# An attention block with a gated feed-forward part: other PSUM banks, another split of the score maxima and another place for the query projections in its first query block

## The chip, the core and the metric

The kernel runs on one core of a Trainium2 chip. The metric is the device time of one execution in microseconds (us), lower being better. A profiled execution also leaves a trace of every instruction: PE is the matrix engine (PEld its weight loads), DVE the vector engine, ACT the activation engine, POOL the general engine, SP the engine that issues the DMAs.

## The reference, cut to what matters

```python
mod = (silu(c) @ w_mod).reshape(1, 6, 1, -1)          # sa, ca, ga, sb, cb, gb
h = layernorm(x) * (1 + ca) + sa                      # x: 1 x 2048 x 512
q = h @ wq   # 32 heads of 16;   k = h @ wk, v = h @ wv: one head of 16 for all
p = softmax(q @ k.T * 16 ** -0.5)
x = x + ga * ((p @ v) @ wo)
h = layernorm(x) * (1 + cb) + sb
x = x + gb * ((sigmoid(h @ w_gate) * (h @ w_up)) @ w_down)    # 512 -> 1792 -> 512
```

## The kernel before, in words

The 2048 queries are cut into 4 blocks of 512 (`b`). A block has 8 units (`u`), each of four heads, so there are 32 units; a unit has 16 steps, one for each 128 keys, so there are 512 steps (`s` in the main loop). Two kinds of score tiles are made, both 128x512 in a PSUM bank:

- `st` tiles (`st_tile`): 128 keys by 512 queries, four to a step, one for each head. ACT takes the exponential of each into `P`. The softmax maximum is already in them: rows of `qp` and `kp` hold it, so it has to be known before the unit starts.
- `sa` tiles (`a_tile`): 128 queries by 512 keys, 64 to a unit, four to a step. DVE takes the maximum of each row into `mx`. They run 76 tiles ahead (`A0`): the maxima of unit i+1 are made during unit i. After a unit's last one, `max_end` and `max_rows` bring the 16 maxima of a row together, transpose them and send them by DMA to DRAM (`mD`) and back into rows of `qp`.

`pv` multiplies `P` by the values (with a column of ones for the sum), two halves to a step, into the bank `c`. A matmul of an `st` tile uses one half of the array's rows and the `sa` tile beside it the other half, so the two run at once.

There are three stages. The **prologue** loads and normalises x, projects keys and values, makes the six modulation vectors (`pmod`, `pcol`, `prow`) and the maxima of the first unit; its order is the list `PLAN` (`q02` is the query projection of block 0, third group of eight heads; `a5` is "sa tiles up to 20"; `z3` makes modulation vector 3), but a scheduler may still move its instructions. Then comes the **main loop** of 512 steps, where instructions keep the order in which they are written. In its first 128 steps, the first query block, `light` alone decides what stands between the score tiles; after that `fill` does, with a planner that keeps a clock for each engine (`COST`, `READ`, `HALF`) and puts pairs of half-height matmuls of other work (`Couple`) where the planned clock leaves room: the attention output projection (`po`), the transposes, gate and up (`pgu`) and down (`pd`) of the block before. `pick` takes them from `main`, or from `spare`, which goes ahead of `pgu` and `pd`. What is left over is done in the **tail**, with the feed-forward part of the last block, by matmuls over the whole array (`alone`).

In the prologue's unit 0 the maxima are made by positive parts (`both`): of two key tiles a and b, PE makes a-b (keys `kd`, the differences) and b, ACT takes the positive part of a-b into `rl`, and DVE adds b and takes the maximum, since max(a, b) = b + max(a-b, 0). Everywhere else DVE takes a plain maximum of each tile.

A query projection (`q_group`) is 12 matmuls with 512 columns. Two of the 16 are made in the prologue. The other 14 are made as 7 couples in steps 2 to 120, one or two pairs of matmuls at `n % 4 == 1` of a step. Their results go to DRAM (`qD`), and from there into `qp`.

DMAs that are `paced` are taken from a list, `queue`, at most one at every second score tile; `later` appends to it. Weights (`split_weight`) are loaded through it, cut into two float16 parts by POOL, and kept or stored (`wD`). The eight PSUM banks are, in the first block: `c`, two for `st`, two and every third time a third (`c2`) for `sa`, and two for couples (`b`).

Of the kernel before, what the change touches and what calls it, by code (L numbers as in the profile page):

```python
# [9 lines left out]
F32 = mybir.dt.float32  # L10
# [17 lines left out]
NU = 8  # L28
# [7 lines left out]

PLAN = 'n1 x2 l0 k0 x3 t1 l3 e1 w0 l1 n2 w3 k1 w1 q00 n3 q01 t2 t3 e2 e3 l2 m a1 k2 a3 k3 a5 w2 a8 z3 a12 z4 a16 z2 a18 z5'

# [11 lines left out]
WSTEPS = 120  # L50
WLAST = 124

# [10 lines left out]
SWITCH = 0.84  # L63
QSKIP = 2
WAIT = 0.2
OVER = 4

PBUFS = 4
SBANKS = {"st": 2, "sa": 2}
GWB = 3  # L70
RBUFS = 4
HBUFS = 36
# [3 lines left out]
def adaln_mqa_glu_kernel(  # L76
# [25 lines left out]
    psum = {}  # L102
    coarse, third = [], [0]
    psum["ctx"] = ExitStack()
# [4 lines left out]


    def bank(name):
        return psum["b"].tile([P, 512], F32, tag="b", name=name, bufs=psum.get("n", 7))

    def sbank(name):
        if name == "sa" and coarse:
            third[0] = (third[0] + 1) % 3
            if third[0] == 0:
                return cbank2("c2")
        return psum["s"].tile([P, 512], F32, tag=name, name=name, bufs=SBANKS[name]) if "s" in psum else bank(name)

# [3 lines left out]
    def cbank2(name):  # L124
        return psum["b"].tile([P, 512], F32, tag="c2", name=name, bufs=1)

# [173 lines left out]

    def split_weight(src, hi, lo, shape):
# [15 lines left out]
        later("w", lambda: load(0), lambda: load(1), split)  # L317

# [109 lines left out]
    def passes(ah, al, bh, bl):  # L428
        return ((ah, bh), (ah, bl), (al, bh))
# [102 lines left out]
    def a_tile(i, n):  # L532
        qp, pr0 = get_q(i)
        if i not in mxs:
            mxs[i] = wp.tile([P, 4, 4, 4], F32, tag="mx", name="mx", bufs=2)
            if i == 0:
# [165 lines left out]


    def weight_jobs():
        jobs = []
# [18 lines left out]
        for k in [*range(4, NFC), *range(4)]:  # L724
            jobs.append(lambda k=k: split_weight(w_down[k * P:(k + 1) * P, :], lambda: wdh[:, k], lambda: wdl[:, k], [D]))
        return jobs
# [15 lines left out]
    def ffn_groups(b):  # L742
# [116 lines left out]
        def down_group(t, lo):  # L859
            def term(n, rs):  # L860
                f, i = lo + n // 3, n % 3
                g_, w_ = passes(*gT[f], wdh, wdl)[i]
                return g_[rs, t * P:(t + 1) * P], w_[rs, f, :]
# [92 lines left out]
    psum["s"] = psum["ctx"].enter_context(tc.tile_pool(name="pa", bufs=1, space=PSUM, reuse_waits="tile"))  # L956
    psum["b"], psum["n"] = psum["s"], 6 - sum(SBANKS.values())
    pinned.append(True)
# [38 lines left out]

    banks = {"st": [0.0, 0.0], "sa": [0.0, 0.0, 0.0]}
    vq = []
# [45 lines left out]


    def light(n):
        if n % 4 == 1:
            c_, k = divmod(n // 4 - QSKIP, 17)
            if n // 4 >= QSKIP and c_ < len(early):  # L1050
                ats = [0, *(12 * (z + 1) // 9 for z in range(9)), *(12 + 12 * (z + 1) // 8 for z in range(8))]
                clock["pe"] += ats[k + 1] - ats[k]
                ready(READ - 1)
                early[c_].part(ats[k], ats[k + 1])
        elif n % 2 == 0 and vq and NKB * vq[0][0] + vq[0][1] <= n // 4 - LAG - (n % 4 == 0):
            clock["pe"] += SWITCH
            do_pv()

    def fill(n):
        if n < 4 * NU * NKB:  # L1060
            return light(n)
        if coarse:
            coarse.clear()
            banks["sa"].pop(0)
        while True:
# [15 lines left out]
    for i, (b, u) in enumerate(units):  # L1081
# [4 lines left out]
        for kb in range(NKB):  # L1086
# [45 lines left out]
    psum["b"] = psum["ctx"].enter_context(tc.tile_pool(name="pz", bufs=1, space=PSUM, reuse_waits="tile"))  # L1132
    psum["n"] = 7
    del psum["s"]
# [42 lines left out]
```

## Time and profile before

| | |
|---|---|
| time, median of 3 runs | 1740.71 us (1738.91 to 1744.54) |
| profiled execution, its own time | 1734.11 us |
| its span, first to last instruction | 1732.3 us |
| mean granted clock of TensorE | 0.984 |
| PE busy | 1650.6 us (95%) |
| DVE busy | 1462.8 us (84%) |
| ACT busy | 1293.4 us (75%) |
| POOL busy | 589.9 us (34%) |

A busy share is an average over the stages, so it tells little by itself. The views that matter are those of one stage: the busy times of a stretch, and the instructions of an engine in order of time, where the distance from one start to the next tells what a step costs.

### The profile page before, as it was taken

The numbers are of one execution on the slowest core, as the hardware profiler recorded it, in microseconds if no ns is written. First come the engines' busy times: TensorE is split into PE (matmuls) and PEld (weight loads), VectorE is DVE, ScalarE is ACT, GpSimd is POOL, SyncE is SP. The second block draws the span as 40 slices with busy tenths as digits, with TensorE's granted clock in tenths as the row PEclk, the third lists the DMA queues.
The fourth block names the chain that finished last, engine by engine and source line by source line (L and its number), as shares of the span: only waits on it lengthen the run. The fifth ranks groups of instructions, "written<-read, shape, count | busy, mean of one in ns | idle before, by whom it ended". The sixth has DMA issues, their size and how long they took to land.

```text
span 1732.3 us, 91155 instructions
## 1 busy us (share of the span) xinstructions
PE 1650.6 (95%) x41276; PEld 966.7 (56%) x41276; DVE 1462.8 (84%) x2490; ACT 1293.4 (75%) x2265; POOL 589.9 (34%) x654
## 2 busy tenths in 40 slices
PE   5889999999899999999999999999999999999998
PEld 3323333232455776767766767777657776654443
DVE  8589999999999999999899999999999999953211
ACT  3668888788878888888778888888888888885100
POOL 4303444444364321331353322332263222230433
PEclk9779999999999999999999999999999999999999
DMA  7002222322302110110202110110212110121211
GB/s 262 28 25 62 84 87 83 89 90 67 83 21 61 48 33 20 44 49 8 72 22 61 51 33 27 39 39 17 63 34 57 45 32 24 45 58 40 75 59 49
DMA packets 112284, 94.76 MB, mean 55 GB/s; under 512 B 27296, under 2 KB 102560, under 8 KB 111896
## 3 DMA queue, kind: packets, MB, share of 16 engines
q1 hardware_dynamic: 111896, 88.94, 17.2%
q8 instruction: 323, 5.29, 1.3%
q14 instruction: 65, 0.53, 0.1%
HBM read 67.95 MB, written 16.48 MB: 49 GB/s over the span
## 4 chain that ended last, share of the span: by engine, by line
PE 79%; DVE 9%; ACT 5%; issue 4%; DMA 2%; POOL 1%; SPq 1%; POOLq 0%; ACTq 0%; DVEq 0%
PE c L137 24%; PE st L137 15%; PE pgu L137 12%; PE sa L137 10%; DVE mx L137 5%; PE pd L137 5%; PE pgu L195 4%; ACT P L137 3%; PE pd L195 3%; PE pq L137 2%; PE po L137 1%; PE sa L175 1%; PE pmod L278 1%; DVE mm L137 0%; POOL ot L875 0%
## 5 line engine op out<-in xcount | busy, mean ns | idle before, releaser
L137 ACT ACTIVATE P<-st 128x512 f32<-128x512 f32 x2048 | 1181.5, 597 | 246.1 <-PE st L137 100.4
L137 DVE TENSOR_REDUCE mx<-sa 128x1 f32<-128x512 f32 x1802 | 1172.8, 687 | 71.5 <-PE sa L137 39.0
L137 PE MATMUL st<-qp,kp 64*32 64x512 f16 (+1 forms) x6656 | 864.7, 379 | 19.6 <-ACT P L137 8.5
L137 PE MATMUL sa<-kp,qp 64*32 64x512 f16 (+1 forms) x6182 | 768.8, 380 | 14.5 <-DVE mx L137 8.5
L137 PE MATMUL c<-P,V 64*32 64x256 f32 (+1 forms) x14336 | 706.2, 380 | 3.9 <-issue 2.9
L137 PEld LDWEIGHTS <-kp 64*32 64x32 f16 (+1 forms) x6656 | 275.7, 92 | 258.8 <-issue 172.4
L137 PEld LDWEIGHTS c<-P,V 64*32 64x32 f32 (+1 forms) x14336 | 324.9, 106 | 136.3 <-issue 92.7
L137 PEld LDWEIGHTS <-qp 64*32 64x32 f16 (+1 forms) x6352 | 302.3, 90 | 120.5 <-issue 52.9
L137 PE MATMUL pgu<-h2h,gw 64*32 64x512 f16 x5248 | 290.5, 377 | 2.0 <-issue 1.1
L137 PEld LDWEIGHTS <-gw 64*32 64x32 f16 x7872 | 163.3, 92 | 51.2 <-issue 19.0
L137 PE MATMUL pgu<-h2l,gw 64*32 64x512 f16 x2624 | 170.2, 377 | 0.8 <-issue 0.5
L846 POOL TENSOR_SCALAR th<-th 128x512 f32<-128x512 f32 x41 | 25.3, 617 | 368.9 <-ACT th L137 357.9
L137 DVE TENSOR_REDUCE mx<-c 128x1 f32<-128x512 f32 x170 | 116.0, 683 | 4.2 <-PE c L137 3.8
L313 POOL TENSOR_SCALAR wst<-wst 128x512 f32<-128x512 f32 x46 | 28.4, 618 | 200.4 <-DMA wst<-in_B_w_gate_dram 78.0
L508 POOL MEMSET qp<- 32x2048 f16 x32 | 57.6, 1799 | 86.2 <-PE st L137 66.0
L137 PE MATMUL pd<-wdl,gh 64*32 64x512 f16 x1120 | 78.3, 377 | 0.7 <-issue 0.7
L137 PE MATMUL pd<-wdh,gh 64*32 64x512 f16 x1120 | 78.4, 377 | 0.0
L137 PE MATMUL pd<-wdh,gl 64*32 64x512 f16 x1120 | 76.1, 376 | 0.0
L869 POOL TENSOR_TENSOR ot<-ot,gb 128x512 f32<-128x512 f32 x10 | 12.8, 1281 | 173.6 <-ACT ot L137 173.5
L195 PE MATMUL pgu<-h2h,gw 128*128 128x512 f16 x240 | 71.8, 379 | 0.0
L840 ACT ACTIVATE th<-pgu 128x512 f32<-128x512 f32 x15 | 9.0, 597 | 80.8 <-PE pgu L195 80.8
L137 PE MATMUL c<-kp,qp 64*128 64x512 f16 x170 | 66.2, 389 | 1.1 <-DVE mx L137 1.1
(173 smaller groups left out, 1467.2 us busy)
## 6 DMA issues: line engine op xcount, KB each, us to landing
gw<-wD SPq DMA_DIRECT2D x224, 128.0 KB
wD<-gw SPq DMA_DIRECT2D x56, 128.0 KB
wm<-in_w_mod_dram SPq DMA_DIRECT2D x6, 1024.0 KB
qp<-qD SPq DMA_DIRECT2D x96, 64.0 KB
xall<-in_A_x_dram SPq DMA_DIRECT2D x4, 1024.0 KB
qD<-q SPq DMA_DIRECT2D x32, 128.0 KB
raw<-cs SPq DMA_DIRECT2D x128, 32.0 KB
xr<-in_A_x_dram SPq DMA_DIRECT2D x32, 128.0 KB
```

The source lines that it names most:

```text
L137: return keep(f_(out_, *a, **k))
L175: pe.matmul(out_[cut], l_[:, cut], r_, start=start, stop=stop)
L195: pe.matmul(self.bank, l_, r_, start=(n == 0), stop=(n == self.n - 1))
L278: pe.matmul(p_[32 * k:32 * (k + 1)], cbc[:, k, :], wmods[i][:, k, :], start=True, stop=True)
L313: pool.tensor_scalar(w_, w_, SW, 0.0, op0=ALU.mult, op1=ALU.add)
L508: pool.memset(qp[j:j + 32], 0.0)
L840: act.activation(th, p_, AF.Tanh, scale=0.5 / (SH * SW))
L846: pool.tensor_scalar(th, th, 1.0, 1.0, op0=ALU.add, op1=ALU.mult)
L869: pool.tensor_tensor(ot, ot, mods2['gb'], op=ALU.mult)
```

## The change

In the first block the banks are shared out again: `st` turns through three of them and `sa` through four, and none is left for couples. After that block the numbers are as before (two for `st`, two for `sa`, one `c2`, two for couples).

Units 1 to 8, whose maxima are made in the prologue's end and in the first block, use positive parts for a quarter of the pairs of tiles (`h == qt`).

Six more query projections are in the prologue's list. The other eight are four couples in `spare`, taken by the planner behind the first block; the branch in `light` that placed the seven couples is gone.

`later` puts weights and output stores behind all else in `queue`, and `need` takes out only what it was asked for. The last four pieces of `w_down`, which lie where the query weights are, are asked for when all 16 projections are stored, not from step 124 on.

```diff
-PLAN = '... a1 k2 a3 k3 a5 w2 a8 z3 a12 z4 a16 z2 a18 z5'
+PLAN = '... a1 k2 a3 k3 a5 w2 a7 q02 a9 z3 q03 a11 z4 q10 a13 q11 z2 a15 q12 a17 q13 a18 z5'
-SBANKS = {"st": 2, "sa": 2}
+FIRST = {"st": (0, 1, 2), "sa": (3, 4, 5, 6)}
+RINGS = {"st": (0, 1), "sa": (3, 4), "c2": (5,), "f": (6, 2)}
+LAST = ("w", "out")
...
+    def ring(name, tags):
+        at[name] = (at.get(name, -1) + 1) % len(tags)
+        t_ = tags[at[name]]
+        return psum["b"].tile([P, 512], F32, tag=f"x{t_}", name=name, bufs=1)
...
     def sbank(name):
+        if not pinned:
+            return bank(name)
+        return ring(name, FIRST[name] if coarse else RINGS[name])
...
-            queue.extend((tag, f_) for f_ in fs)
+            n = len(queue) if tag in LAST else sum(z[0] not in LAST for z in queue)
+            queue[n:n] = [(tag, f_) for f_ in fs]
     def need(tag):
-        while any(z[0] == tag for z in queue):
-            queue.pop(0)[1]()
+        for z in [z for z in queue if z[0] == tag]:
+            queue.remove(z)
+            z[1]()
...
-        both = i == 0
+        both = i == 0 or i <= NU and h == qt
...
-    early = [Couple(q_group(*z), q_group(*y)) for z, y in zip(qleft[::2], qleft[1::2])]
-    main, spare = [], []
+    main, spare = [], [Couple(q_group(*z), q_group(*y)) for z, y in zip(qleft[::2], qleft[1::2])]
...
     def light(n):
-        if n % 4 == 1:
-            c_, k = divmod(n // 4 - QSKIP, 17)
-            if n // 4 >= QSKIP and c_ < len(early):
...
-                early[c_].part(ats[k], ats[k + 1])
-        elif n % 2 == 0 and vq and ...:
+        if n % 2 == 0 and vq and ...:
             do_pv()
...
-                if wdone >= nw - 4 and s < WLAST + 3 * (wdone - nw + 4):
+                if wdone >= nw - 4 and len(qdone) < 4 * NB:
                     break
```

PE in an early step of the first block, before; `wdh` and `wdl` are the two parts of the query weights there, `h1h` the normalised input:

```order
L137 MATMUL st<-qp,kp 128x512
L137 LDWEIGHTS qp
L137 MATMUL sa<-kp,qp 128x512
L137 LDWEIGHTS wdl
L137 MATMUL pq<-h1h_215,wdl 128x512
L137 LDWEIGHTS wdl
L137 MATMUL pq<-h1h_215,wdl 128x512
L137 LDWEIGHTS wdh
L137 MATMUL pq<-h1h_221,wdh 128x512
L137 LDWEIGHTS wdh
L137 MATMUL pq<-h1h_221,wdh 128x512
L137 LDWEIGHTS kp
```

The same place of the changed program; `kd` marks a tile of differences:

```order
L141 MATMUL c<-P_1286,V 32x256 x2
L141 MATMUL c<-P_1299,V 32x256 x2
L141 LDWEIGHTS kp
L141 MATMUL st<-qp,kp 128x512
L141 LDWEIGHTS qp
L141 MATMUL sa<-kd,qp 128x512
L141 LDWEIGHTS kp
L141 MATMUL st<-qp,kp 128x512
L141 LDWEIGHTS qp
L141 MATMUL sa<-kp,qp 128x512
```

The one or two pairs of `pq` matmuls of a step are gone, the score tiles and `pv` stand as they did, and one `sa` tile in eight is made of differences.

DVE in the first block, before; `c_1154` and its like are the tiles in the third bank of the maxima:

```order
L137 TENSOR_REDUCE mx<-sa 128x1 x2
L137 TENSOR_REDUCE mx<-c_1154 128x1
L137 TENSOR_REDUCE mx<-sa 128x1 x2
L137 TENSOR_REDUCE mx<-c_1173 128x1
L137 TENSOR_REDUCE mx<-sa 128x1 x2
```

The same place of the changed program; `ISA junk,mx` adds the positive part and takes the maximum, and the row behind it reads its result out:

```order
L141 TENSOR_REDUCE mx<-sa 128x1 x9
L141 ISA junk,mx<-sa,rl 128x512
L141 ISA mx 128x1
L141 TENSOR_REDUCE mx<-sa 128x1 x5
L141 ISA junk,mx<-sa,rl 128x512
L141 ISA mx 128x1
L141 TENSOR_REDUCE mx<-sa 128x1 x5
```

Of eight tiles DVE now takes six plain maxima and one of the longer kind; the eighth is ACT's, as `rl`.

PE in the prologue behind modulation vector 4, before:

```order
L278 MATMUL pmod<-wm,cbc 32x512 x4
L288 MATMUL pcol<-sel,mod 128x1 x4
L175 LDWEIGHTS qp
L175 MATMUL sa<-kd,qp 128x512
L175 LDWEIGHTS qp
```

The same place of the changed program:

```order
L284 MATMUL pmod<-wm,cbc 32x512 x4
L294 MATMUL pcol<-sel,mod 128x1 x4
L201 LDWEIGHTS wdh
L201 MATMUL pq<-h1h_358,wdh 128x512
L201 LDWEIGHTS wdh
L201 MATMUL pq<-h1l_359,wdh 128x512
L201 LDWEIGHTS wdl
```

A whole query projection, 12 matmuls over the full array, stands ahead of the next `sa` tiles.

More of the change, by code (lines that the diff above doesn't have):

```diff
@@ L102, in adaln_mqa_glu_kernel @@
     psum = {}
-    coarse, third = [], [0]
+    coarse, at = [], {}
     psum["ctx"] = ExitStack()
@@ L106, in adaln_mqa_glu_kernel @@
     dr = ctx.enter_context(tc.tile_pool(name="dr", bufs=1, space=DRAM))
+    def ring(name, tags):
+        at[name] = (at.get(name, -1) + 1) % len(tags)
+        t_ = tags[at[name]]
+        return psum["b"].tile([P, 512], F32, tag=f"x{t_}", name=name, bufs=1)
     def bank(name):
-        return psum["b"].tile([P, 512], F32, tag="b", name=name, bufs=psum.get("n", 7))
+        return ring("f", RINGS["f"]) if pinned else psum["b"].tile([P, 512], F32, tag="b", name=name, bufs=7)
     def sbank(name):
[L115 to L119, printed above, removed]
+        if not pinned:
+            return bank(name)
+        return ring(name, FIRST[name] if coarse else RINGS[name])
     def cbank(name):
@@ L124, in cbank2 @@
     def cbank2(name):
[L125 removed]
+        return ring("c2", RINGS["c2"])
     class Ordered:
@@ L298, in mod_rows, with split_weight @@
         return g_
-    def split_weight(src, hi, lo, shape):
+    def split_weight(src, hi, lo, shape, *more_):
         w = []
@@ L315, in split @@
             pool.tensor_tensor(lo_, w_, hi_, op=ALU.subtract)
-        later("w", lambda: load(0), lambda: load(1), split)
+        later("w", lambda: load(0), lambda: load(1), split, *more_)
     def row_norm(dsts, srcs, later=False):
@@ L700, in gw_tile @@
         return P2.tile([P, 4, NDC, P], F16, tag="gw", name="gw", bufs=GWB)
+    loaded = []
     def weight_jobs():
@@ L724, in weight_jobs @@
         for k in [*range(4, NFC), *range(4)]:
-            jobs.append(lambda k=k: split_weight(w_down[k * P:(k + 1) * P, :], lambda: wdh[:, k], lambda: wdl[:, k], [D]))
+            jobs.append(lambda k=k: split_weight(w_down[k * P:(k + 1) * P, :], lambda: wdh[:, k], lambda: wdl[:, k], [D],
+                                                   lambda: loaded.append(k)))
         return jobs
@@ L861, in term @@
                 f, i = lo + n // 3, n % 3
+                assert len(loaded) == NFC
                 g_, w_ = passes(*gT[f], wdh, wdl)[i]
@@ L996, in free @@
         return max(clock[z] for z in keys) + FREE
-    banks = {"st": [0.0, 0.0], "sa": [0.0, 0.0, 0.0]}
+    banks = {z: [0.0] * len(FIRST[z]) for z in FIRST}
     vq = []
@@ L1047, in light @@
     def light(n):
-        if n % 4 == 1:
-            c_, k = divmod(n // 4 - QSKIP, 17)
-            if n // 4 >= QSKIP and c_ < len(early):
-                ats = [0, *(12 * (z + 1) // 9 for z in range(9)), *(12 + 12 * (z + 1) // 8 for z in range(8))]
-                clock["pe"] += ats[k + 1] - ats[k]
-                ready(READ - 1)
-                early[c_].part(ats[k], ats[k + 1])
-        elif n % 2 == 0 and vq and NKB * vq[0][0] + vq[0][1] <= n // 4 - LAG - (n % 4 == 0):
+        if n % 2 == 0 and vq and NKB * vq[0][0] + vq[0][1] <= n // 4 - LAG - (n % 4 == 0):
             clock["pe"] += SWITCH
@@ L1063, in fill @@
             coarse.clear()
-            banks["sa"].pop(0)
+            for z in banks:
+                banks[z] = banks[z][-2:]
         while True:
```

9 lines of the change are left out of this document (3 added, 6 removed).

## The prediction

> **What bounds the kernel now.** I read the page first, then the busy times by stage, then PE, ACT and DVE in order of time inside the stage that changes.
>
> ```profile
> PE 1650.6 (95%) x41276; PEld 966.7 (56%) x41276; DVE 1462.8 (84%) x2490; ACT 1293.4 (75%) x2265; POOL 589.9 (34%) x654
> ```
>
> Stretches follow, with the busy time of PE, PEld, DVE, ACT and POOL, the granted clock, the DMA share and GB/s: the first projections, the cold part of the prologue, the first block (from the first exp of step 0 to that of step 128), the next 32 steps, and the other 352.
>
> ```profile
> 28.50:52.40 23.90, 17.13 (x177) 11.15 (x175) 16.61 (x32) 14.09 (x23) 13.82 (x12) 1.00 0.35 116
> ...
> 72.90:100.20 27.30, 24.04 (x86) 7.50 (x85) 17.78 (x54) 13.01 (x24) 0.00 (x0) 0.50 0.01 1
> 104.20:448.40 344.20, 334.01 (x3404) 104.70 (x3407) 329.89 (x558) 288.57 (x526) 146.04 (x170) 0.98 0.25 76
> 448.40:544.60 96.20, 88.23 (x2633) 54.38 (x2633) 89.75 (x150) 78.30 (x138) 45.24 (x61) 1.00 0.19 52
> 544.60:1580.00 1035.40, 1007.48 (x34075) 705.63 (x34059) 934.62 (x1520) 860.00 (x1492) 314.49 (x330) 1.00 0.14 40
> ```
>
> In the first block PE is busy 97%, DVE 96% and ACT 84% of 344.2 us. Busy shares so close together don't say which engine sets the step, so I go down to single steps. ACT in order of time, where a row is the four exps of a step:
>
> ```profile
> 202.88 2.22 ACT L137 ACTIVATE P<-st 128x512 f32<-128x512 f32 x4 [0.24 <-PE c L137]
> ...
> 223.10 2.30 ACT L137 ACTIVATE P<-st 128x512 f32<-128x512 f32 x4 [0.29 <-PE sa L137]
> ```
>
> Eight steps lie between these rows: 20.22 / 8 = 2.53 us a step. 128 steps at that rate are 323.5; the other 20.7 of the 344.2 are waits, most of them where units meet. PE in one of these steps, which holds a single pair of query matmuls:
>
> ```profile
> 202.45 0.39 PE L137 MATMUL st<-qp,kp 64*128 64x512 f16 x1
> ...
> 204.91 0.39 PE L137 MATMUL st<-qp,kp 64*128 64x512 f16 x1
> ```
>
> That is 2.46. Seven couples have 168 pairs in 119 steps, so 1.41 a step; with 0.22 a pair (row below) the mean is 2.46 + 0.41 x 0.22 = 2.55, which is what I measured. PE sets the step while queries are in it. The last pairs stand in step 120, before 430 us, and PE and ACT behind them look so:
>
> ```profile
> 430.07 0.39 PE L137 MATMUL st<-qp,kp 64*128 64x512 f16 x1
> ...
> 430.52 0.37 PE L137 MATMUL st<-qp,kp 64*128 64x512 f16 x1
> ...
> 432.52 0.39 PE L137 MATMUL st<-qp,kp 64*128 64x512 f16 x1
> ```
> ```profile
> 429.38 2.19 ACT L137 ACTIVATE P<-st 128x512 f32<-128x512 f32 x4 [0.31 <-PE sa L137]
> ```
>
> Without queries a step is still 2.45 (430.07 to 432.52). The second `st` matmul waits to 430.52: with two banks it needs the one that the second exp of the row at 429.38 reads. That exp starts 0.49 after the first (below), at 429.87, and is through at 430.47. DVE in that place:
>
> ```profile
> 428.94 1.28 DVE L137 TENSOR_REDUCE mx<-sa 128x1 f32<-128x512 f32 x2
> 430.14 0.68 DVE L137 TENSOR_REDUCE mx<-c 128x1 f32<-128x512 f32 x1
> 430.74 1.28 DVE L137 TENSOR_REDUCE mx<-sa 128x1 f32<-128x512 f32 x2
> ```
>
> Three maxima take 1.80, so 0.60 each and 2.40 a step. The step thus has three limits side by side: PE with queries 2.46 to 2.68, two banks for exps 2.45, DVE 2.40. The change moves all three.
>
> **First block, by its parts.** *PE*: without queries a step needs 2.46 - 0.22 = 2.24. *Banks*: the third bank for `st` takes away the wait of 0.2 above. *DVE* now has six plain maxima and one positive part in two steps. The trace has positive parts only in the prologue:
>
> ```profile
> 75.98 0.69 DVE L551 CUSTOM_DVE_ANT_0 junk<-sa,rl 128x512 f16<-128x512 f32 x1 [0.17 <-DVE mx L551]
> 76.60 0.08 DVE L551 DVE_READ_ACCUMULATOR2_ANT mx<- 128x1 f32 x1
> 76.86 0.69 DVE L551 CUSTOM_DVE_ANT_0 junk<-sa,rl 128x512 f16<-128x512 f32 x1 [0.17 <-PE pmod L278]
> ...
> 96.60 0.69 DVE L551 CUSTOM_DVE_ANT_0 junk<-sa,rl 128x512 f16<-128x512 f32 x1 [0.17 <-ACT mod L280]
> 97.22 0.08 DVE L551 DVE_READ_ACCUMULATOR2_ANT mx<- 128x1 f32 x1
> 97.33 0.22 DVE L565 TENSOR_REDUCE m<-mx 128x16 f32<-128x64 f32 x1
> ```
>
> One costs 0.88 ahead of another of its kind, and 0.73 ahead of something else (96.60 to 97.33). In the new order plain maxima stand between them, so I take 0.73: 6 x 0.60 + 0.73 = 4.33 for two steps, 2.17 a step (2.24 with 0.88). *ACT* has eight exps and one positive part in two steps. Rows for its rate, a pair of exps, a lone one, six positive parts, and 38 exps near the end:
>
> ```profile
> 201.55 1.08 ACT L137 ACTIVATE P<-st 128x512 f32<-128x512 f32 x2 [0.31 <-PE sa L137]
> ```
> ```profile
> 477.42 0.60 ACT L137 ACTIVATE P<-st 128x512 f32<-128x512 f32 x1 [2.01 <-PE st L137]
> ```
> ```profile
> 79.99 3.21 ACT L549 ACTIVATE rl<-sa 128x512 f32<-128x512 f32 x6 [2.50 <-PE sa L175]
> ```
> ```profile
> 1554.38 21.84 ACT L137 ACTIVATE P<-st 128x512 f32<-128x512 f32 x38 [0.32 <-PE st L137]
> ```
>
> One exp lasts 0.60 and the second of a pair starts 1.08 - 0.60 = 0.48 to 0.49 behind the first. Positive parts come every (3.21 - 0.60) / 5 = 0.52. So ACT needs 8 x 0.49 + 0.52 = 4.44, or 2.22 a step, if nothing holds it up. The 38 exps came every 21.84 / 38 = 0.57, which is the other end: 2.59 a step. They had two banks, so I put them down to the banks.
>
> PE 2.24, ACT 2.22 and DVE 2.17 lie so close that none runs smoothly. I walked two steps by hand. PE issues score pairs at 0, 0.23, 1.12 and 1.35 and so on, and an exp starts 0.43 behind its matmul (202.45 and 202.88 above). With the positive part behind the first two exps, ACT takes up the third at 1.93 instead of 1.55, and frees that bank at 2.53, where PE wants it at 2.47, with a semaphore to wait for; about 0.2 is lost in two steps. That gives 4.47 + 0.2 = 4.67, **2.33 a step**. The waits where units meet stay at 20.7: DVE's end of a unit and the row of maxima sent through DRAM last as long as before. 128 x 2.33 + 20.7 = 318.9, **25 less** than 344.2. Bounds: 2.24 a step (37 less), 2.59 (8 more).
>
> The page "ScalarE: Activation LUTs" of the Trainium skill, in the section "What ACT_TABLE_LOAD costs", speaks against this step: it gives an ACTIVATE with immediate operands as 186 ns + 0.833 ns an element, less 93 ns of overlap, an estimate of 0.52 for 512 elements. By that ACT's nine in two steps would set the pace and most of the gain would go. This trace's pairs of exps are faster (0.49), its positive parts agree (0.52).
>
> **Prologue.** Six projections of 12 matmuls are added. Three rows: two `pmod` with a stretch of 16 maxima between them, and ten matmuls of the projections that the prologue has already, from the chain of waits.
>
> ```profile
> 74.84 1.93 PE L278 MATMUL pmod<-wm,cbc 128*32 128x512 f32 x8
> ...
> 84.38 1.94 PE L278 MATMUL pmod<-wm,cbc 128*32 128x512 f32 x8
> ```
> ```profile
> 38.89 2.16 PE pq L195 x10
> ```
>
> At the full clock a matmul is 0.216, a projection 2.6, six 15.6; at half clock twice as much, 31. The stretch of 9.54 ran at a clock of 0.50. Its own work would be about 4.8 at the full clock, and two projections would make it 10.0, or 0.5 more than now; at half clock 10.4 more. So the six cost between 2 and 31. The projections at 38.89 ran at a clock of 1.00 (first stretch above), since such matmuls are dense; I take a quarter of the way up, **8 more**. ACT has 14 and POOL 27 us free there, which hides their two copies and one subtraction each; SP has nothing else to issue there than the maxima's rows, which come behind them, so the 12 stores stay hidden.
>
> The page "TensorE: Matmul & The Clock Gate" of the Trainium skill (Part 1) says that the clock is full after about 3.4 us of busy matmuls. Here PE was busy 24.04 of 27.30 us and still had 0.50, so the trace disagrees as far as busy time goes. By that rule alone this term would be 2 and the forecast 1721.
>
> **Behind the block.** The changed order has three of the four couples at steps 127 to 142 and the last at 151 to 154; the output projection begins at step 142 instead of 137. If all 72 pairs that do not reappear elsewhere came on top, they would cost 72 x 0.216 = 15.6. But PE has room there: its feed-forward work is not ready yet, and it even waits on its way, at 469 for a DMA, so that ACT stood 2.01 idle (row at 477.42).
>
> ```profile
> 469.38 5.18 DMA rb<-lD
> ```
>
> With the couples these 32 steps carry the load of the later ones, which are 1035.4 / 352 = 2.94 each; 32 x 2.94 = 94 against 96.2 now. **2 less**, bounds 6 less (that wait gone with the later start) and 15.6 more. From step 160 on the couples of a step are the same ones, shifted by 24 pairs: nothing. These 24 are one couple of `pgu`, which is left for the tail, where PE works alone:
>
> ```profile
> 1597.64 13.61 PE pd L195 x63
> ```
>
> 24 x 13.61 / 63 = **5 more**. The reordered queue I cost at nothing: the gate and up weights are asked for by step 120 and read from 159 on, and the last of `w_down` have 40 steps. If that cover were gone, each late piece would cost a DMA's time, as at 469.38. New waits in DVE and ACT are for each other's positive parts; behind ACT's stand the exps, which the walk above has counted.
>
> **Sum.** 8 - 25 - 2 + 5 = -14. The profiled execution took 1734.1 (span 1732.3 and 1.8 around it) and would take 1720; the median of the runs is 6.6 higher, 1740.7, so I forecast **1727**.
>
> **The rivals.**
> - *ACT becomes the bound, slower.* If 0.57 is ACT's own rate, a step is 4.5 x 0.575 = 2.59, the block costs 8 more and the whole is 8 + 8 - 2 + 5 = 19 more: 1760. It decides from 2.44 a step on, where the block's gain of 11 is eaten by the other terms. For it speaks the row of 38 exps, against it the pairs at 0.49.
> - *The prologue stays cold.* 31 - 25 - 2 + 5 = 9 more: 1750. For it the clock of 0.50 now, against it the dense projections.
> - *Exps come at the rate of positive parts.* With nine ACT instructions at 0.52 two steps need 4.68, with the 0.2 lost 4.88, so 2.44 a step; the block gains 11, and 8 - 11 - 2 + 5 = 0: 1741. The same comes out if three engines within 0.07 of one another hold each other up and a step falls only to 2.46, as in the steps without queries. For it the row of six positive parts, against it again the pairs. (The ScalarE page's figure, above, leads here.)
> - *All goes smoothly.* 2.24 a step, 2 for the prologue, 4 less behind the block: 2 - 37 - 4 + 5 = -34, 1707.
>
> **How the numbers follow.** Forecast 0.54, ACT 0.13, cold prologue 0.10, the slower exps 0.13, all smooth 0.10. The forecast's own range is 1712 to 1742. The range of 8 in 10 reaches from 1705 to 1751: it takes in all but the ACT rival and a little at the ends. A measurement of this kernel tells about 0.3% (5 us) from no change. Faster: forecast and smooth, 0.64. Same: mostly the slower exps, 0.14. Slower: ACT and cold prologue, 0.22.
>
> **What would show it.** The first exp should come near 112 instead of 104.6; groups of exps and positive parts every 4.67 for two steps; the first exp of step 128 near 431; steps 128 to 160 in 94; the tail 5 longer. I am wrong if exps of the first block come no closer than 0.57 on average with ACT never idle, if the clock stays at 0.5 through the projections, or if positive parts of DVE cost 0.88 and hold PE.

## The result, and the profile after

The changed kernel took 1738.5 us (1733.06 to 1748.04, 20 runs) where the kernel before took 1741.39 (1736.12 to 1749.4, 20 runs) beside it: a ratio of 0.9987 with an interval of 0.9972 to 1.0002, so no difference that can be told. A second comparison gave 0.9988 (0.9965 to 1.0011). I had forecast 14 us less; 2 to 3 less was measured (by the ratio and by the medians). The ratios in this document go by the executions in the fast state; one execution of `e8_queue_fifo` (5510.2 us) and one of the kernel before beside the last two kernels (1753.04 us) were slow and are left out.

The profiled execution took 1735.37 us, its span was 1733.6. Its stages, in the columns of the prediction's stretches: the end of the prologue, the first block, the next 32 steps, the other 352, and from the last exp to the end.

```profile
72.90:120.40 47.50, 35.41 (x174) 12.79 (x173) 22.34 (x63) 22.04 (x39) 7.03 (x7) 0.93 0.10 34
120.40:432.40 312.00, 294.53 (x3106) 79.29 (x3112) 286.41 (x548) 295.43 (x581) 124.68 (x149) 0.99 0.25 72
432.40:535.70 103.30, 98.67 (x3172) 65.23 (x3164) 91.09 (x152) 79.86 (x141) 47.53 (x62) 1.00 0.17 50
535.70:1577.00 1041.30, 1012.55 (x34080) 700.09 (x34065) 933.97 (x1520) 858.09 (x1492) 320.48 (x339) 1.00 0.15 41
1577.00:1733.60 156.60, 150.67 (x722) 68.98 (x720) 36.81 (x68) 16.23 (x26) 50.37 (x52) 0.99 0.20 63
```

One profile of each kernel isn't enough to compare stages of this length, as the experiments soon showed. So each kernel was profiled three times; the means and their differences, in us:

| stage | before, three profiles | after, three profiles | difference | forecast |
|---|---|---|---|---|
| first exp | 104.6, 105.9, 104.2 | 120.5, 122.1, 124.3 | +17 | +8 |
| first block | 343.8, 341.1, 341.0 | 312.0, 308.4, 308.8 | -32 | -25 |
| steps 128 to 160 | 96.2, 95.5, 94.9 | 103.2, 100.1, 101.0 | +6 | -2 |
| steps 160 to 512 | 1035.6, 1039.4, 1041.7 | 1041.2, 1043.1, 1027.6 | -2, not told from 0 | 0 |
| last exp to end | 152.2, 152.2, 152.2 | 156.7, 156.7, 156.7 | +4.5 | +5 |

The differences add up to -6, and the three profiled executions are 6 us apart in the mean. The timed runs, of which there are many more, say -2 to -3. The first block gained more than forecast, and the prologue and the 32 steps behind the block took it back.

ACT in a unit of the first block of the changed kernel, in order of time (start, busy time, and no idle time in brackets anywhere):

```profile
206.04 0.59 ACT L141 ACTIVATE rl<-sa 128x512 f32<-128x512 f32 x1
206.51 3.55 ACT L141 ACTIVATE P<-st 128x512 f32<-128x512 f32 x7
209.95 0.60 ACT L141 ACTIVATE rl<-sa 128x512 f32<-128x512 f32 x1
210.42 3.69 ACT L141 ACTIVATE P<-st 128x512 f32<-128x512 f32 x7
214.01 0.59 ACT L141 ACTIVATE rl<-sa 128x512 f32<-128x512 f32 x1
```

From 206.04 to 214.01 there are 14 exps and 2 positive parts without a gap: 7.97 / 16 = 0.498 for each. Two steps hold eight exps and one positive part, so 9 x 0.498 = 4.48, or 2.24 a step. ACT is now the engine that sets the step inside a unit, at 0.50 an instruction. 128 steps of 2.24 are 287; the other 25 of the 312.0 (22 in the other two profiles) lie at the boundaries of units. The waits of PE in that block (engine, line, what it waited for, us in total, times, longest):

```profile
PE st L141 <- DMA qp<-mD: 12.3, 10, 4.5
PE c L141 <- ACT cs L141: 5.8, 7, 0.8
```

The first is the wait for the row of maxima that goes through DRAM, the second the wait for ACT's copy of a unit's sums. The longest wait for the row, 4.5, is the one ahead of the very first score tile and belongs to the prologue; inside the block there are 7.8 us in nine waits, and 4.2 and 6.5 in the other two profiles. The wait for the copy is 5.8 in all three. So neither is clearly the larger.

### The profile page after: what moved, and what is told of

The parts are those of the page before. It is cut to its first block, busy times and chain, and to the rows that moved or that the text cites. A ratio compares the mean times of both kernels' runs of the same rounds, so it can differ in the third digit from the quotient of the medians.

```text
span 1733.6 us, 91980 instructions
## 1 busy us (share of the span) xinstructions
PE 1640.1 (95%) x41612; PEld 954.3 (55%) x41612; DVE 1422.5 (82%) x2487; ACT 1308.3 (75%) x2338; POOL 585.9 (34%) x654
## 4 chain that ended last, share of the span: by engine, by line
PE 82%; DVE 6%; ACT 4%; issue 3%; DMA 2%; POOL 2%; SPq 1%; POOLq 0%; ACTq 0%; DVEq 0%
PE c L141 25%; PE f L141 20%; PE st L141 14%; PE sa L141 11%; PE pgu L201 5%; PE pd L201 3%; DVE mx L141 3%; ACT P L141 2%; DMA qp<-mD 1%; PE pq L201 1%; SPq L586 1%; DVE junk L557 1%; PE po L201 1%; PE pk L444 0%; DMA xall<-in_A_x_dram 0%
## 5 line engine op out<-in xcount | busy, mean ns | idle before, releaser
L141 DVE TENSOR_REDUCE mx<-sa 128x1 f32<-128x512 f32 x1847 | 1196.8, 686 | 96.6 <-PE sa L141 65.7
L141 PE MATMUL st<-qp,kp 64*32 64x512 f16 (+1 forms) x6656 | 848.6, 378 | 24.9 <-DMA qp<-mD 14.6
L141 PE MATMUL sa<-kp,qp 64*32 64x512 f16 (+1 forms) x6290 | 792.7, 379 | 8.1 <-DVE mx L141 5.8
L141 PE MATMUL f<-h2h,gw 64*32 64x512 f16 x5120 | 291.3, 377 | 6.9 <-issue 4.9
L141 PE MATMUL f<-h2l,gw 64*32 64x512 f16 x2560 | 170.4, 376 | 2.4 <-POOL h2l L354 1.1
L141 PE MATMUL f<-wdh,gl 64*32 64x512 f16 x1120 | 74.4, 376 | 0.3
L141 PE MATMUL f<-wdl,gh 64*32 64x512 f16 x1120 | 73.2, 376 | 0.8 <-issue 0.8
L141 PE MATMUL f<-wdh,gh 64*32 64x512 f16 x1120 | 73.4, 377 | 0.0
L861 POOL TENSOR_TENSOR gl<-th,gh 128x512 f16<-128x512 f32 x56 | 65.0, 1161 | 4.7
L860 POOL TENSOR_SCALAR gh<-th 128x512 f16<-128x512 f32 x56 | 34.9, 622 | 88.9 <-DVE th L858 45.4
```

What stands on the lines that cost most here:

```text
L141: return keep(f_(out_, *a, **k))
L860: pool.tensor_scalar(hi, th, 1.0, 0.0, op0=ALU.mult, op1=ALU.add)
L861: pool.tensor_tensor(lo, th, hi, op=ALU.subtract)
```

## The experiments

All ratios are to the kernel before, run beside it on the same chip; the changed kernel stands at 0.9987 and 0.9988. `e10_gate_first`, `e11_two_behind_gate_first` and `p_before3` ran on another chip than the other experiments.

**Which part of the first block's gain comes from what.** `e1_banks_only` makes no positive parts in the first block; `e2_two_exp_banks` keeps those and takes the third bank of `st` away.

```diff
-        both = i == 0 or i <= NU and h == qt
+        both = i == 0
```

> The changed kernel with its seven banks in the first block, but plain maxima everywhere there (positive parts in unit 0 alone). If DVE limits the step once queries and the two-bank wait are gone, a step is four maxima of 0.60, so 2.40 to 2.45 against 2.28 in the changed kernel, the first block is 16 to 20 us longer than its 312, and the whole is 15 to 20 slower than the changed kernel (ratio to before near 1.008). Rival: the banks made the whole gain and ACT is relieved of 64 positive parts; then the block stays at 312 or gets a few us shorter (ratio 0.996 to 0.999).

```diff
-FIRST = {"st": (0, 1, 2), "sa": (3, 4, 5, 6)}
+FIRST = {"st": (0, 1), "sa": (3, 4, 5, 6)}
```

> The changed kernel with two banks for exps in the first block instead of three (four for maxima, positive parts kept). If the loop matmul, exp, free bank limits a step with two banks, steps go back to 2.45, 128 x 0.17 = 22 us more in the block, ratio to before near 1.011. Rival: the two-bank wait was only a sign of DVE running late, and with a quarter of the pairs as positive parts the step stays below 2.33; then 0 to 6 more, ratio 0.999 to 1.002.

Measured: without positive parts 1.0029 (1.0009 to 1.0048), the block 318.7, which is less than the 328 to 332 expected; with two banks for exps 1.0169 (1.0147 to 1.0192), the block 339.9, which is more than expected (a ratio near 1.011). DVE of the first, in order of time, is back to back at 12.68 / 21 = 0.60 a maximum, the 2.40 a step that stood in the kernel before too. The second view is the row of its whole block, in the columns of the stretches above:

```profile
202.57 12.68 DVE L141 TENSOR_REDUCE mx<-sa 128x1 f32<-128x512 f32 x21
```
```profile
123.60:442.30 318.70, 305.64 (x3111) 72.04 (x3118) 314.48 (x547) 281.60 (x519) 125.05 (x149) 0.99 0.24 70
```

DVE is busy 314.5 of 318.7 us: its maxima run on while PE waits at the boundaries, so the boundaries are not added on top of 128 x 2.40 = 307. That is why the block was shorter than expected.

ACT of the second waits for PE in front of every group, and the ten exps between the starts at 206.25 and 212.76 take 6.51, so 2.60 a step, where 2.45 had been expected. The second view has the longest wait of PE in its block:

```profile
206.25 1.71 ACT L141 ACTIVATE P<-st 128x512 f32<-128x512 f32 x3 [0.31 <-PE sa L141]
207.85 0.59 ACT L141 ACTIVATE rl<-sa 128x512 f32<-128x512 f32 x1
208.33 1.66 ACT L141 ACTIVATE P<-st 128x512 f32<-128x512 f32 x3
210.30 2.21 ACT L141 ACTIVATE P<-st 128x512 f32<-128x512 f32 x4 [0.31 <-PE sa L141]
212.76 2.21 ACT L141 ACTIVATE P<-st 128x512 f32<-128x512 f32 x4 [0.24 <-PE sa L141]
```
```profile
PE st L141 <- ACT P L141: 11.0, 35, 0.6
```

PE waits 35 times there for an exp to free a bank; in the changed kernel's first profile that wait is 0.3 us, once.

So without the third bank for exps the block gains only 2 us of the 32 (339.9 against 342 before), although the queries are gone and DVE's maxima cheaper. Without the positive parts it loses 7 to 9 of them (318.7 against 310, and 0.0042 x 1740 = 7 in the timed runs). These shares don't add up to 32, since the limits stood side by side. What the queries cost in the block was not tested: no kernel has them there with three banks.

**What the projections cost in the prologue.** `e3_thin_prologue` issues one matmul instead of twelve for each of the six projections that were added; the rest of their sums is left out.

```diff
-            q_group(*args).alone()
+            g_ = q_group(*args)
+            g_.n = 12 if tok in ('q00', 'q01') else 1
+            g_.alone()
```

> The changed kernel, with only the first of the 12 matmuls in each of the six projections added to the prologue (66 matmuls left out, copies and stores kept). If the projections' own PE time lies on the prologue's path at nearly the full clock, the first exp comes 66 x 0.216 = 14 earlier, near 106 instead of 120.5, and the ratio to before is near 0.990. Rival: they keep the clock up, and without them PE falls back to half clock, or their copies and stores are what costs; then the first exp stays above 112 and the gain is under 8 (ratio 0.994 or more).

Measured: 0.9936 (0.9917 to 0.9955), 9 us less than the changed kernel; the first exp at 116.5. The end of its prologue:

```profile
72.90:116.50 43.60, 33.63 (x111) 9.07 (x109) 23.56 (x65) 22.75 (x42) 7.53 (x8) 0.56 0.11 37
```

The granted clock falls to 0.56 without the dense projections, from 0.93 (0.88 in the other two profiles). Taking out 66 matmuls, 14 us of PE at the full clock, brings the first exp only 4 to 8 earlier, and it stays 12 behind the kernel before. So the projections hold the clock up, as I had assumed, but neither their own time nor the clock alone makes the prologue's 17 us. The positive parts of unit 1 don't either: without them, in `e1_banks_only`, the first exp came at 123.6. What is left to test is the order in which PE's work stands.

`e6_prologue_order` has the same instructions in another order. `y3` makes the four `pmod` matmuls of vector 3 and ACT's copy, `z3` the rest, with a projection between them; `f` ends the first unit's maxima, and two projections follow it.

```diff
-... a7 q02 a9 z3 q03 a11 z4 q10 a13 q11 z2 a15 q12 a17 q13 a18 z5
+... a7 y3 q02 z3 a9 y4 q03 z4 a11 q10 a13 y2 q11 z2 a16 f q12 y5 q13 z5 a18
```

> The changed kernel with the same instructions in the prologue in another order: each projection stands between the four matmuls of a modulation vector and the column or row matmuls that wait for ACT's copy of it, and two projections stand behind the last maximum of the first unit, where the row of maxima is on its way (6.2 us from the transpose to the first score tile in the kernel before). Theory: the prologue's 16 us are the projections' own 16 us at full clock, put into PE's line where DVE's positive parts (0.87 us a pair) cannot cover them; four waits of 0.7 to 1.2 for ACT's copies and the two projections behind the last maximum would be covered, so the first exp comes 6 to 10 us earlier, at 111 to 115 instead of 120.5, and the ratio to before falls from 0.9987 to about 0.994. Rival: the projections are the work of PE that sets the prologue in any order; then the first exp stays within 3 us of 120.5.

Measured: 0.9930 (0.9906 to 0.9953), 10 us less than the changed kernel, the first exp at 112.4. The waits of PE from 70.5 us to the first score tile, in the changed kernel:

```profile
PE st L141 <- DMA qp<-mD: 4.5, 1, 4.5
PE sa L181 <- DVE mx L557: 2.5, 5, 0.8
PE pcol L294 <- ACT mod L286: 2.3, 2, 1.2
PE prow L302 <- ACT mod L286: 1.4, 2, 0.7
```

and in the other order:

```profile
PE sa L181 <- DVE mx L556: 1.6, 4, 0.8
PE st L141 <- DVE mx L558: 1.6, 1, 1.6
PE sa L181 <- ACT rl L554: 1.0, 3, 0.3
PE pmod L284 <- ACT rl L554: 0.9, 3, 0.3
```

The waits for ACT's copies (3.7) and for the row (4.5) are gone, and one of 1.6 ahead of the first score tile has come; the first exp came 8.0 earlier than in the changed kernel's first profile. So the order matters, as the theory says. A later kernel with the same prologue (`e10_gate_first`) had its first exp at 116.7, outside the 111 to 115 expected of this order; its granted clock there was 0.89, against 0.97 here. The changed kernel's two profiles at 0.88 had it at 122.1 and 124.3, so at like clocks the order is worth 5 to 8 us.

The time from one start on PE to the next, summed by kind of instruction over this part, shows the whole account in us. The last wait, from the last `sa` tile to the first score tile, stands by itself:

| | projections | `pmod`, `pcol`, `prow` | `sa` tiles | last wait | sum |
|---|---|---|---|---|---|
| before | 0 | 16.6 | 16.3 | 0.5 | 33 |
| after | 19.4 | 12.0 | 13.3 | 4.9 | 50 |
| other order | 16.4 | 8.5 | 14.6 | 1.9 | 41 |

From the transpose of the maxima to the first score tile it is 6.2 us in the kernel before and 4.7 in the changed one; but before, PE has the last modulation vector and more `sa` tiles to do in that time, and in the changed kernel nothing is left.

**Whether more lead of the maxima removes the boundary waits.** `e5_a0_80` changes one number, `A0 = 76` to 80.

> The changed kernel with the maxima one step further ahead (80 tiles instead of 76), so that the row of maxima of a unit starts one step, some 2.3 us, earlier. Theory 'the row is the wait': in the first block of the changed kernel a step costs 2.28 inside a unit, and the rest, some 12 to 15 us at the seven unit boundaries, is PE waiting for the row that is sent through DRAM (12.3 us in 10 waits in the list of waits). With a step more those waits fall to about 2, the block to about 300 from 312, and the time by 8 to 13 us, to a ratio near 0.992 of before. Rival: DVE and the copy of the sums on ACT end last at the boundary as well; then the waits for the row only change their name, and the block stays within 3 us of 312. The prologue gets four more maxima, which cost 0 to 2 us.

Measured: 0.9970 (0.9949 to 0.9990); the first block 301.8. The waits in its first block:

```profile
PE c L141 <- ACT cs L141: 3.2, 7, 0.5
PE st L141 <- DMA qp<-mD: 1.9, 5, 0.8
```

The waits for the row are 1.9 here and 4.2 to 7.8 inside the block in the changed kernel's profiles, those for the copy 3.2 and 5.8; the block fell by 7 to 10, as expected. But the end from the last exp on took 167.9 instead of 156.7: the planner left one couple more (24 matmuls) for the tail, and PE waited 2.3 there for a gate weight. The first exp at 124.0 and the 1031.1 of steps 160 to 512 lie within the spread of the changed kernel's own profiles. The time fell by 3 us, within the intervals, where 8 to 13 had been expected. `e7_order_and_a0` put both together.

> The prologue's other order and the 80 maxima ahead together. Theory: the two waits lie in different places, so the gains add: first exp near 113 to 115 (112.4, and four maxima more), first block 300 to 303, the ratio to before 0.003 to 0.006 below the 0.993 of the order alone, so 0.987 to 0.990. Rival: the step gained at the boundaries is given back by more pairs of feed-forward matmuls left for the tail (it grew by 11 with 80 maxima alone, while steps 160 to 512 fell by 10); then the ratio is 0.991 to 0.994.

Measured: 0.9956 (0.9932 to 0.9980), no better than the order alone, and outside both ranges expected. Its tail was as long as that of `e5_a0_80` (167.8). Its first exp was at 119.4, with the clock at 0.87 in the end of the prologue and 3.6 us of waiting for DVE's extra maxima ahead of the first score tile. The gains didn't add.

**What the couples cost behind the block.** `e4_thin_behind` gives the couples of `q` matmuls with 128 columns instead of 512, except the first of each projection; three quarters of these projections' columns lack all but their first term.

```diff
-                    mm(g.bank, l_, r_, n == 0, n == self.n - 1)
+                    few = slice(0, 128 if self.stage == 'q' and n > 0 else 512)
+                    mm(g.bank[:, few], l_, r_[:, few], n == 0, n == self.n - 1)
```

> The changed kernel in the same order, but the matmuls of the four couples of projections behind the first block, all but each one's first, have 128 columns instead of 512; 92 pairs are some 0.16 shorter, 14.7 us of PE time. If steps 128 to 160 have about 10 us of idle PE time that swallows part of the couples (st and sa matmuls took 43.0 us of PE there before, 33.1 in the changed kernel), only the part above that comes back: 7 us, 103 to 96, ratio to before near 0.994. Rival: PE is full there and all 14 come back (ratio 0.990). Other rival: POOL, the weights' DMA or the order is what made these steps longer, and nothing comes back (ratio 0.998 to 0.999).

Measured: 0.9952 (0.9932 to 0.9971), 6 us less than the changed kernel, but steps 128 to 160 took 101.4, like the changed kernel's mean. The couples' time on PE there (start to start) fell from 21.8 to 16.2; what PE gained it spent waiting (start to start, its `st` tiles rose from 17.9 to 22.3). So in this profile PE's own work doesn't set that stage. The DMAs in the order in which SP issued them show one candidate. Before:

```profile
515.61 18.95 SPq L165 DMA_DIRECT2D gw<-wD  x12
```

After:

```profile
520.26 4.77 SPq L171 DMA_DIRECT2D qD<-q  x4
526.04 0.32 SPq L581 DMA_DIRECT2D mD<-mt  x1
527.48 2.83 SPq L586 DMA_DIRECT2D qp<-mD  x4
530.41 8.82 SPq L171 DMA_DIRECT2D gw<-wD  x7
```

The loads of the gate weights stand behind the last couple's stores and behind the row of maxima, and start 5 us ahead of step 160 (535.7), where they started 29 us ahead of it before (544.6). PE waited for them at step 159, which took 5.3 us:

```profile
PEld L141 <- DMA gw<-wD: 2.9, 3, 1.1
```

Two kernels test the list. `e8_queue_fifo` undoes the change's own rule on where new DMAs are put (`need` stays as changed):

```diff
-LAST = ("w", "out")
+LAST = ()
```

> The changed kernel with its list of paced DMAs in order of arrival again, weights and output stores no longer behind the rest. Theory: the list's order has cover and is worth nothing: ratio within 0.002 of the changed kernel's, all stages within their spread. Rival: without it the loads of the gate weights, which already end the wait of 2.7 us at step 159, and the loads of queries stand behind weights, and steps 128 to 160 take 2 us or more longer.

Measured: 1.0043 (1.0023 to 1.0063), some 10 us slower than the changed kernel. The rival was right on the kind of wait, with another place and size: steps 160 to 176 took 57.9 instead of 48. Eight gate loads are issued, and then weights of `w_down` stand ahead of the next ones, which start at 560.16.

```profile
526.70 10.20 SPq L171 DMA_DIRECT2D gw<-wD  x8
538.45 0.82 SPq L171 DMA_DIRECT2D wst<-in_B_w_down_dram  x2
...
543.54 10.90 SPq L171 DMA_DIRECT2D wst<-in_B_w_down_dram  x5
...
560.16 2.16 SPq L171 DMA_DIRECT2D gw<-wD  x4
```

PE's wait for them in that kernel, from 530 to 592:

```profile
PE f L141 <- DMA gw<-wD: 9.6, 4, 4.6
```

So the rule on the list, which I had costed at nothing, is worth some 10 us once the couples stand behind the block. The other kernel, `e10_gate_first`, goes on from `e6_prologue_order` and puts the stores of queries at the end of the list too:

```diff
-            n = len(queue) if tag in LAST else sum(z[0] not in LAST for z in queue)
+            last = lambda z: z in LAST or z[0] == "q"
+            n = len(queue) if last(tag) else sum(not last(z[0]) for z in queue)
```

> The prologue's other order, and in the list of paced DMAs the stores of queries stand at its end too, so that five loads of gate weights are issued ahead of the row of maxima of unit 9 and not behind it. Theory 'the gate weights come late': PE's waits for them at steps 158 to 160 (2.7 to 5 us) go, unit 9 (steps 144 to 160) falls from 54 to 48 to 50, steps 128 to 160 from 101 to 95 to 97, and the ratio by about 0.003 from 0.993, to 0.990. Rival 'PE is full there': the pairs that waited are done a little later or earlier, PE's work in units 9 and 10 stays the same and only moves between them; the ratio stays at 0.992 to 0.994.

Measured: 0.9897 (0.9866 to 0.9928). Five gate loads now start ahead of the row:

```profile
510.44 5.95 SPq L172 DMA_DIRECT2D gw<-wD  x5
517.45 0.32 SPq L581 DMA_DIRECT2D mD<-mt  x1
518.89 2.84 SPq L586 DMA_DIRECT2D qp<-mD  x4
```

No wait for gate weights is left, steps 144 to 160 took 50.6 instead of the 54.6 of `e6_prologue_order`, and steps 160 to 176 47.3 instead of 49.5. That is 6 us in the two units; steps 128 to 160 took 98.3, where 95 to 97 had been expected. The ratio fell by 0.0033, but its interval still meets that of `e6_prologue_order`, and it was measured on the other chip.

`e9_two_more_behind` moves two of the six projections (q12, q13) out of the prologue of `e6_prologue_order` into a fifth couple, and `e11_two_behind_gate_first` adds the list of `e10_gate_first` to it.

> The kernel with the prologue's other order, with two of the six projections (q12, q13) moved from the prologue behind the first block: a fifth couple, 24 more pairs. Theory 'PE is full behind the block': the pairs cost their own time there, 24 x 0.227 = 5.4 more in steps 128 to 160 or, where work shifts, in the stages behind; the first exp comes 2 to 4 earlier (5.2 us of matmuls less, of which the row on its way covered a part), so the time is equal or up to 4 us worse than with the order alone: ratio 0.993 to 0.996. Rival, as in the prediction: PE has room behind the block, the pairs cost 0 to 2 there, and the ratio falls to about 0.991.

> The same change of the list in the kernel with two more projections behind the block, where the gate and up matmuls begin behind step 160 already and no wait for their weights shows. Theory: no change, the ratio stays within 0.002 of 0.993. If the list's order is worth something without that wait (stores that hold up SP), it falls by more.

Measured: 0.9929 (0.9899 to 0.9958) and 0.9900 (0.9863 to 0.9936). In `e9_two_more_behind` steps 128 to 160 took 95.5, not 106, though 24 pairs had come in: the gate matmuls began behind step 160 and didn't wait. So the pairs don't cost their own time in these steps; whether they cost it in the stages behind, as the expectation allowed, is hidden by the spread of those stages. The first exp came at 111.7, hardly earlier than 112.4, and as a whole two projections cost the same in either place. `e11_two_behind_gate_first` was the control: it has no such wait to lose, and its ratio fell by 0.003 all the same. Both kernels with the new list ran on the other chip, so these 0.003 may be the chip's. So the wait for gate weights, gone from the trace, isn't shown in the timed runs.

**The spread of the last stage.** `p_before2`, `p_before3`, `p_after2` and `p_after3` are the two kernels again.

> The kernel before, profiled once more, for the spread of the stages from one profile to the next. Steps 160 to 512 took 1035.5 us in its one profile and 1041 to 1049 in five profiles of kernels with the changed code there. If the change makes those steps slower, they come out at 1033 to 1038 again; if it is the spread of profiles, at 1040 to 1048. First exp 104.6, first block 343.8 and steps 128 to 160 96.1 should come back within 2 us.

> The changed kernel, profiled once more, for the same purpose: first exp 120.5, first block 312.0, steps 128 to 160 103.3, steps 160 to the end of the exps 1041.3 in its one profile. If profiles of one kernel agree, each comes back within 2 us; if they spread, the first block comes out at 307 to 316 and the last stage at 1036 to 1049.

> The changed kernel once more, for its time beside the others on the same chip and a third profile. Ratio to before 0.997 to 1.000; first exp 120 to 122, first block 308 to 312, steps 128 to 160 100 to 103, steps 160 to the end of the exps 1041 to 1046, tail 156.7.

> The kernel before, a third profile: the time from the first exp of step 128 to the end, 1283.9 and 1287.0 so far, against 1285 to 1301 in three profiles of the changed kernel and 1294 to 1310 in four others with its code there. If the change costs about 15 us behind the block, it comes out at 1281 to 1290; if that stage only spreads by 25 us from profile to profile, at up to 1300.

Their stages stand in the table above. Steps 160 to 512 of the changed kernel's third profile, with the same number of PE's matmuls as the first:

```profile
534.10:1561.70 1027.60, 1003.36 (x34080) 701.04 (x34060) 932.71 (x1520) 858.74 (x1492) 320.55 (x339) 1.00 0.15 42
```

That is 13.7 less than in its first, and outside the 1041 to 1046 expected. In `e1_banks_only` to `e3_thin_prologue`, whose code is the same from there on, the stage took 1046 to 1049. The 6 us by which the first two profiles differ there can't be told from this spread. From step 128 to the end the kernel before took 1283.9, 1287.0 and 1288.7, the changed one 1301.1, 1299.9 and 1285.2, so a cost of 15 us behind the block isn't shown either.

## Why the prediction was wrong, step by step

*Reading of the first block: right as far as it was tested.* PE, two banks for exps and DVE were said to stand at nearly the same step. `e1_banks_only` brings DVE's limit back at the 2.40 that the rows of before gave. `e2_two_exp_banks` brings back that of the banks, but at 2.60: more than the 2.45 read at 430 us, and what the row of 38 exps gave for nine instructions in two steps (2.59). PE with the queries in the block, the third limit, was brought back by no run.

*Its size: 7 too small.* The walk put 0.2 of loss on top of 4.47 for two steps. There was next to none: ACT ran without a gap, and two steps took 4.48 against ACT's floor of 4.44. The step was 0.09 shorter than forecast, 11 us in 128, and the boundaries took 25 where 20.7 was kept. The rival in which ACT becomes the bound was right on the engine and wrong on the rate: 0.50 an instruction, not 0.57, so it set the step only just above the other floors. The Trainium skill's page "ScalarE: Activation LUTs" (section "What ACT_TABLE_LOAD costs") leads to the estimate of 0.52 that I had quoted; the trace's 0.50 lies between it and the 0.49 of pairs.

*Prologue: +17 for +8, the largest miss.* The step that failed is "its own work would be about 4.8 at the full clock". I took the stretch of 9.54 for PE's own work at half clock, which halves when the clock rises. The clock did rise, to 0.93, but the work that was there before fell only from 32.9 to 25.3: `pmod`, `pcol` and `prow` gained 4.6 of their 16.6, and the `sa` tiles 3.0 of their 16.3. A pair of `sa` tiles takes DVE 0.87 to 0.88 from start to start in both kernels, at either clock. Another 4.4 came at the end: the last two projections stood ahead of the row that the first score tile needs, and PE had nothing left to do while the row was on its way. And some projections ran at half clock (19.4 for the 15.6 of the full one). That makes 19.4 - 7.6 + 4.4 = 16. With the other order the same instructions cost 8, or 12 with a lower clock. How much each moved piece of that order brings was not tested. (A quarter of the way from 2 to 31 would also have been 9, not 8.) The Trainium skill's page "TensorE: Matmul & The Clock Gate" (Part 1) was nearer on the clock than my row: the dense projections raised it. But its forecast of +2 was still further off, since about half of the work there did not follow the clock.

*Behind the block: +6 for -2.* The step that failed is "with the couples these 32 steps carry the load of the later ones". In the changed kernel PE spends 39.8 us there on couples, transposes and the first gate matmuls (start to start), against 32.5 in a mean of 32 steps later on, which is 7 more than the 94 I took. That this load is the cause isn't shown: with 5.6 us of it taken away, in `e4_thin_behind`, the stage took 101.4, the changed kernel's mean. The traces show one other cause, the wait for gate weights, with step 159 at 5.3 us where it took 3.0 to 3.3 in the kernel before. And the cover that I named for these weights, from step 120 to step 159, was read off their stores and not off their loads back, which wait for the list and for the row of maxima. The rest of the 8 stays open.

*The list of DMAs: wrong.* Nothing was the wrong price. In the changed program its rule is worth some 10 us, which the couples behind the block would otherwise have cost on top.

*Steps from 160 on, and the tail.* For the steps nothing was forecast and 2 less measured, which the spread of 15 us within one kernel can't tell from nothing. The tail was right to 0.5 us, three times.

The forecast missed by 12. The terms behind it: prologue 9 and steps 128 to 160 8 more, the first block 7 less, steps 160 to 512 2 less, and 4 between the profiles' -6 and the timed -2. That the miss isn't 19 is luck: the first block's extra gain covered a part of it. The result lies nearest to the rival with 1741, whose reason (the slower rate of exps) was not the one.

What stays open is how much a pair of query matmuls costs behind the block. `e4_thin_behind` says 6 us for all, by timed runs alone; `e9_two_more_behind` shows no cost for a quarter more of them.

## What to carry to other kernels

When work is moved out of a stage that is full, price its new places by what ends last there: in this prologue DVE's 0.88 a pair and the row on its way as much as the matrix engine's clock; behind the block a load that stands in a list behind other DMAs (10 us in `e8_queue_fifo`). The same six projections cost 17 us in one order and 8 to 12 in another, so the order in which a moved piece is set between a producer and the one that waits for it can be worth more than the piece. And profile each kernel more than once before a few us of a long stage are explained.

The kernel with the other order and the queries' stores last in the list has the lowest ratio of those run, 0.9897 (0.9866 to 0.9928); `e11_two_behind_gate_first` (0.9900) and the order alone (0.9930) can't be told from it.

## What the runs showed of the hardware that was not expected

- The positive part and maximum on DVE costs less between plain maxima than in the prologue: the next maximum starts 0.61 behind it where the prologue's rows gave 0.73 and 0.88. DVE of the changed kernel in the first block:

```profile
207.89 0.69 DVE L141 CUSTOM_DVE_ANT_0 junk<-sa,rl 128x512 f16<-128x512 f32 x1
208.50 0.08 DVE L141 DVE_READ_ACCUMULATOR2_ANT mx<- 128x1 f32 x1
208.50 1.28 DVE L141 TENSOR_REDUCE mx<-sa 128x1 f32<-128x512 f32 x2
```

- 14 exps and 2 positive parts came every 0.50 us on ACT with no gap.
- The granted clock in the end of the prologue was 0.50 before, 0.93 (0.88 in two more profiles) with 72 dense matmuls more, and 0.56 with six of these 72. With PE's instructions there in the same other order it was 0.97 in one kernel (`e6_prologue_order`) and 0.89 in another (`e10_gate_first`).
- Steps 160 to 512 with the same instructions took from 1027.6 to 1049.1 us in seven profiles (three of the changed kernel, and `e1_banks_only` to `e4_thin_behind`), at a granted clock of 1.00.
